# Weighted expert groups: a seven-product scheme for the first product, and matmuls in 64x64 pieces on two halves of the rows

## The chip, the cores and the metric

The kernel runs on one core of one Trainium2 chip. The metric is device time in microseconds, the median of the runs. The engines are TensorE (PE in the profile: matmuls, with their weight loads as PEld), VectorE (DVE), ScalarE (ACT), GpSimd (POOL) and SyncE (SP), which issues most DMAs.

## What is computed

An attention block with polynomial features makes `x` (4352 rows of 128). Then a mixture of eight experts works on it, with weights `P` from eight rounds of row and column normalisation. All of it is fp32.

```python
    logits = x @ w_gate
    ...
    for _ in range(8):
        P /= P.sum(1, keepdims=True) + 1e-09
        P /= P.sum(0, keepdims=True) + 1e-09
        P *= N / E
    out = np.zeros((N, D), dtype=np.float32)
    for e in range(E):
        h = np.maximum(x @ w1[e], 0.0)
        ye = h @ w2[e]
        out += P[:, e:e + 1] * ye
```

Here N = 4352, D = 128, E = 8, and the hidden width F = 1024. Two matrix products for each expert take nearly all the time: the first is `x @ w1[e]`, the second `h @ w2[e]`. As P is not negative, `P * relu(x @ w1)` is `relu((P * x) @ w1)`: a weighted group multiplies x by P ahead of the first product and then sums over the experts in PSUM.

## The kernel before

**Layout.** `xT` holds x transposed: 128 features on the partitions, tokens along the free axis. The first product puts hidden units on the partitions, the second puts output features there.

**Groups, items, blocks.** `groups` is a list of (first token, tile width, tiles, experts, weighted). The eight groups ahead of `PLAIN` are unweighted, two tiles wide, for experts 0 and 1; they run beside the attention and the routing. Then come five weighted groups of three tiles of 256 tokens (`NT3`), for experts 1 to 7 (the group at token 512: 2 to 7), and a last weighted group of two tiles. An *item* is a group with one expert. An item of a three-tile group has two *blocks*; a block is four of the eight slices of 128 hidden units. There are 34 such items and 68 such blocks; they are the three-tile stage, from 184.9 to 830.0 us.

**A three-tile block** (`four`, `twenty`). `first` (L906 to L920) makes, for each slice, two matmuls of 128x64 weights, one for each half of the array's columns, with 512 or 256 tokens, into one bank of PSUM, and ScalarE stores the relu to `hx` or `hb` in turn (L920). `sums` has VectorE form thirteen sums and differences of these slices (L980, L1000). The second product is a scheme of 20 products of half blocks of W2 and of 256 tokens in place of 24: `twenty` lists them, and `into` (L1107) adds them into four banks of PSUM over all experts of the group. The 16 needed sums of half blocks of W2 are made by GpSimd in the first weighted group (`sums_of_four`, L242), stored in DRAM, and loaded by the later groups.

**Order.** For PE, DVE and ACT the order is written out by hand: `steps` emits, for each step of a block, one `first`, then the sums that are due, then the second products of a block begun eight steps earlier (`LAG`). So first and second products alternate on PE. GpSimd's and SP's work is kept in program order where `keep_in_program_order` says so.

**Inputs of an item.** `prepare_x` loads the row of P for the expert, repeated on all partitions (a DMA from `pT`, L674), and GpSimd multiplies it with x into `xe` (L678). `prepare_w` loads W1, W2 and the forms of W2. Both run one item ahead.

**End of a group.** When a bank is complete, ScalarE copies it out (L820), and `part_of_twenty` combines the four copies: 23 additions on VectorE (`do`, L823), five copies between halves on ScalarE (L842), three transposes (L714), and the stores.

Of the kernel before, what the change touches and what calls it, by code (L numbers as in the profile page):

```python
# [10 lines left out]
F32 = mybir.dt.float32  # L11
# [39 lines left out]
def kernel(  # L51
# [32 lines left out]
    sk = ctx.enter_context(tc.tile_pool(name="sk", bufs=2))  # L84
# [5 lines left out]
    early = ExitStack()  # L90
    ld = early.enter_context(tc.tile_pool(name="ld", bufs=2))
# [94 lines left out]

    def load_w(e, sums=True, again=False):
# [6 lines left out]
    def sums_of_two(e, w2, again=False):  # L194

        ws = wpool.tile([P, 4, FO // 2, H2], F32, tag="ws", name="ws")
# [27 lines left out]
    FORMS = [n for ns, *_ in FOURS for n in ns]  # L224

    def sums_of_four(e, w2):
# [6 lines left out]
        def blocks(bs):  # L233
            b = w2[:, bs[0][1]::4, H2 * bs[0][0]:H2 * (bs[0][0] + 1)].unsqueeze(1)
            if len(bs) == 1:
                return b
            step = (bs[1][1] - bs[0][1]) * DM + (bs[1][0] - bs[0][0]) * H2
            return AP(tensor=b.tensor, offset=b.offset, ap=[b.ap[0], [step, 2], *b.ap[2:]])
# [10 lines left out]


# [320 lines left out]
    def routing():  # L571

        yield 5
# [52 lines left out]
    lower, upper = slice(0, H2), slice(H2, P)  # L626
# [28 lines left out]
    def prepare_w(j):  # L655
        g, e = items[j]
        three = groups[g][2] == 3
        if j == 0:
            loaded_w[j] = first_w
        elif items[j - 1][1] == e or not groups[g][4]:  # L660
            before = [i for i in range(j) if items[i][1] == e and i in loaded_w]
            loaded_w[j] = loaded_w[before[-1]] if before else load_w(e, False)
            if three and tiles_of(j - 1) == 2:
                loaded_w[j] = *loaded_w[j][0:2], sums_of_four(e, loaded_w[j][1])
        else:
            loaded_w[j] = load_w(e, not three, again=groups[g][4])
            if three:
                if g == len(groups) - 2 and e in groups[-1][3]:
                    sums_of_two(e, loaded_w[j][1], True)
                loaded_w[j] = *loaded_w[j][0:2], sums_of_four(e, loaded_w[j][1])  # L670
# [9 lines left out]
    def prepare_x(j):  # L680
# [3 lines left out]
        if not weighted:  # L684
            sources[j] = x
            return
        xe = weights_of(e, lo, t * n, "xe")
        for sl in (slice(0, 512), slice(512, 768)) if j == first_weighted else (slice(0, t * n),):
            weigh(xe[:, sl], x[:, sl], xe[:, sl])
        sources[j] = xe  # L690
# [123 lines left out]
    def part_of_twenty(g, k):  # L814
# [7 lines left out]
        def do(out, a, b, off=False):  # L822
            at_leisure(lambda: nc.vector.tensor_tensor(out, a, b, op=Alu.subtract if off else Alu.add))  # L823
# [12 lines left out]
        elif k == 3:  # L836
# [51 lines left out]
    def room_of(k):  # L888

        lo, n, t, _, weighted = groups[items[blocks[k][0]][0]]  # L890
        if t == 3:
            if "x" not in hs:
                hs["x"] = pools[0].tile([P, 25, NT3], F32, name="hx", bufs=1)
                hs["pqg"] = pools[0].tile([P, 3, NT3], F32, name="pqg", bufs=1)
# [59 lines left out]
    U4, U2, V3, V1, U1, V4, W1, W2, U3, BB, V2, W3, W4 = range(12, 25)  # L954

    def four(k):
        j, q = blocks[k]
        h = hs[k] = room_of(k)
        pqg = hs["pqg"]
        order = ((0, 0), (3, 0), (3, 1), (0, 1), (1, 0), (2, 0), (1, 1), (2, 1))  # L960

        def at(f, t):
            return 4 * t + f

        def step(c):
            f, last = order[c]
            if last:
                first(k, 4 * q + f, 2 * NT3, 3 * NT3, h[:, at(f, 2)], False)
            else:
                first(k, 4 * q + f, 0, 2 * NT3, h[:, f:f + 8:4], False)  # L970

        def places(*bs):
            if len(bs) == 1:
                return h[:, bs[0]]
            if bs[0] == bs[1]:
                return h[:, bs[0]:bs[0] + 1].to_broadcast([P, 2, NT3])
            return h[:, bs[0]:bs[1] + 1:bs[1] - bs[0]]

        def do(out, a, b, off=False):
            nc.vector.tensor_tensor(out if not isinstance(out, tuple) else places(*out), places(*a),  # L980
                                    places(*b) if isinstance(b, tuple) else b, op=Alu.subtract if off else Alu.add)

# [296 lines left out]
```

## Time and profile before

| | |
|---|---|
| median of the runs | 919.61 us (2 runs: 919.25 and 919.96) |
| the profiled execution: span from its first to its last instruction | 917.7 us |
| three-tile stage, 68 blocks | 184.9 to 830.0 us |
| granted TensorE clock | 1.00 throughout |
| DMA | 128 MB, 140 GB/s on average |

A row of the page's groups and of the list by form reads: line, engine, operation, written tile <- read tiles, partitions x elements, count, then busy us, mean ns of one, and idle time of the engine just before. A row of the timeline: start, length, engine, line, operation, tiles, shape, count of merged instructions, and in brackets the idle time before and what ended it. A row of a table by stretch: the stretch, its length, then for each engine its busy time and its number of instructions, the granted clock, the DMAs' share and their rate. The row of one tile's or line's instructions has the shortest, median and longest duration in ns. Every fp32 matmul shows as two records.

### The profile page before, as it was taken

To read this page: it belongs to the slowest core of one execution; us is meant where nothing else is said; L and a number is where in the kernel's file an instruction comes from. 1 tells how busy PE (TensorE), PEld (TensorE's weight loads), DVE (VectorE), ACT (ScalarE), POOL (GpSimd) and SP (SyncE) were. 2 spreads that over 40 slices of the span, in tenths; PEclk is the share of its full clock that TensorE was granted. 3 is DMA by queue.
4 is the path that set the end of the run, shared out by engine and by line. 5 is a ranking of instruction groups with operands and counts; after the bars stand their busy time and mean duration, and the time that the engine had idled before them with its cause. 6 is when DMAs were issued, how large, how long until landed. Compare 5 with 4: busy or idle time off the path is not lost.

```text
span 917.7 us, 18881 instructions
## 1 busy us (share of the span) xinstructions
PE 910.4 (99%) x7434; PEld 695.8 (76%) x7434; DVE 687.7 (75%) x1173; ACT 422.7 (46%) x918; POOL 210.4 (23%) x212
## 2 busy tenths in 40 slices
PE   9999999999999999999999999999999999999997
PEld 6777544466666688888888888888888888888997
DVE  7678699888876798766975666966667987678654
ACT  3355465554444454444544444544445444446443
POOL 3121100175545422200210011110100352340110
PEclk9999999999999999999999999999999999999999
DMA  9994100213445545534364343463434556552550
GB/s 250 307 276 165 54 1 1 70 64 110 161 142 152 172 133 158 182 110 146 115 173 148 110 150 110 122 200 120 140 113 165 148 161 190 164 192 92 150 158 13
DMA packets 91305, 128.15 MB, mean 140 GB/s; under 512 B 25392, under 2 KB 69504, under 8 KB 86480
## 3 DMA queue, kind: packets, MB, share of 16 engines
q1 hardware_dynamic: 88384, 121.42, 43.0%
q0 software_dynamic: 1600, 5.36, 2.0%
q8 instruction: 58, 0.95, 0.4%
q10 hardware_dynamic: 1232, 0.16, 0.1%
q14 instruction: 31, 0.25, 0.1%
HBM read 107.88 MB, written 19.05 MB: 138 GB/s over the span
## 4 chain that ended last, share of the span: by engine, by line
PE 96%; DVE 2%; ACT 1%; DMA 1%; issue 0%; SPq 0%; DVEq 0%; ACTq 0%
PE a L916 51%; PE s L1107 41%; PE a L347 1%; PE a L462 1%; DMA kx<-in_k_dram 1%; DVE hb L933 1%; PE a L314 0%; PE s L376 0%; PE a L426 0%; PE s L392 0%; DVE cs L602 0%; PE a L496 0%; PE a L392 0%; ACT hb L920 0%; DVE rs L596 0%
## 5 line engine op out<-in xcount | busy, mean ns | idle before, releaser
L916 PE MATMUL a<-xe,w 128*64 128x256 f32 (+1 forms) x2560 | 615.4, 470 | 0.0
L916 PEld LDWEIGHTS a<-xe,w 128*64 128x64 f32 x2560 | 306.3, 137 | 39.2 <-issue 1.6
L920 ACT ACTIVATE hb<-a 128x256 f32<-128x256 f32 (+4 forms) x408 | 195.1, 480 | 241.7 <-PE a L916 210.9
L1107 PE MATMUL s<-hb,ws 128*64 128x256 f32 (+3 forms) x1312 | 276.4, 395 | 0.2 <-DVE hb L933 0.2
L920 ACT ACTIVATE hx<-a 128x256 f32<-128x256 f32 (+1 forms) x360 | 167.3, 465 | 211.6 <-PE a L916 194.6
L1107 PE MATMUL s<-hx,ws 128*64 128x256 f32 x1280 | 253.6, 379 | 0.0
L1107 PEld LDWEIGHTS s<-hb,ws 128*64 128x64 f32 x1312 | 161.5, 137 | 67.9 <-issue 14.7
L980 DVE TENSOR_TENSOR hb<-hb 128x512 f32<-128x512 f32 (+1 forms) x204 | 138.3, 687 | 97.9 <-ACT hb L920 93.8
L678 POOL TENSOR_TENSOR xe<-xT,xe 128x768 f32<-128x768 f32 (+2 forms) x41 | 84.0, 2050 | 490.5 <-DMA xe<-pT 363.6
L1107 PEld LDWEIGHTS s<-hx,ws 128*64 128x64 f32 x1280 | 159.6, 137 | 48.3
L980 DVE TENSOR_TENSOR hx<-hx 128x512 f32<-128x512 f32 (+1 forms) x204 | 149.0, 741 | 59.1 <-ACT hx L920 54.1
L1107 PE MATMUL s<-hb,w 128*64 128x256 f32 (+3 forms) x536 | 120.3, 408 | 0.0
L916 PE MATMUL a<-xT,w 128*64 128x416 f32 (+3 forms) x512 | 119.9, 462 | 0.0
L1107 PE MATMUL s<-hx,w 128*64 128x256 f32 x384 | 81.8, 379 | 0.0
L933 DVE TENSOR_TENSOR hb<-hb 128x416 f32<-128x416 f32 (+7 forms) x84 | 59.9, 713 | 19.4 <-ACT hb L920 15.8
L1107 PEld LDWEIGHTS s<-hb,w 128*64 128x64 f32 x536 | 60.0, 137 | 17.4 <-issue 6.5
L916 PEld LDWEIGHTS a<-xT,w 128*64 128x64 f32 x512 | 49.5, 137 | 25.0 <-issue 15.6
L242 POOL TENSOR_TENSOR ws<-w 128x256 f32<-128x256 f32 (+1 forms) x70 | 61.1, 907 | 8.1 <-DMA w<-in_moe_w_dram 8.0
L933 DVE TENSOR_TENSOR hx<-hx 128x256 f32<-128x256 f32 (+1 forms) x65 | 37.2, 576 | 25.4 <-ACT hx L920 24.2
L1107 PEld LDWEIGHTS s<-hx,w 128*64 128x64 f32 x384 | 46.4, 137 | 4.4
L980 DVE TENSOR_TENSOR pqg<-hb 128x512 f32<-128x512 f32 x68 | 43.2, 676 | 0.0
L980 DVE TENSOR_TENSOR pqg<-hx 128x512 f32<-128x512 f32 x68 | 37.7, 594 | 0.0
(180 smaller groups left out, 489.8 us busy)
## 6 DMA issues: line engine op xcount, KB each, us to landing
w<-in_moe_w_dram SPq DMA_DIRECT2D x82, 512.0 KB, 5.5
ws<-ws SPq DMA_DIRECT2D x34, 1024.0 KB, 4.9
xe<-pT SPq DMA_DIRECT2D x34, 384.0 KB, 4.0
ws<-ws SPq DMA_DIRECT2D x12, 512.0 KB, 3.1
ph<-qa SPq DMA_DIRECT2D x12, 288.0 KB, 4.8
rb<-qb SPq DMA_DIRECT2D x3, 1152.0 KB, 7.6
pb<-pT SPq DMA_DIRECT2D x6, 384.0 KB, 8.6
kx<-in_k_dram SPq DMA_DIRECT2D x4, 544.0 KB, 5.0
```

The source lines that it names most:

```text
L242: tc.keep_in_program_order(nc.gpsimd.tensor_tensor(ws[:, c:c + len(ns)], blocks(x), blocks(y), op=Alu.subtract if off else Alu.add))
L347: nc.tensor.matmul(pv[64 * s:64 * (s + 1), i], kp[0:n, H * t + h].rearrange("p i j -> p (i j)"), vx[0:n, slots[h], t, :], start=(t == 0 an ...
L462: nc.tensor.matmul(pn[64 * s:64 * (s + 1), t, 2 * i:2 * i + 2].rearrange("p h d -> p (h d)"), ph[:, i, s, 64 * t:64 * (t + 1)], kvs[b % 2] ...
L678: tc.keep_in_program_order(nc.gpsimd.tensor_tensor(out, x, pb, op=Alu.mult))
L916: nc.tensor.matmul(ph[sl], loaded_w[j][0][:, P * f + H2 * s:P * f + H2 * (s + 1)], sources[j][:, lo:hi], start=True, stop=True, tile_posit ...
L920: nc.scalar.activation(out=out, in_=ph, func=Act.Relu)
L933: nc.vector.tensor_tensor(out, a, b, op=Alu.subtract)
L980: nc.vector.tensor_tensor(out if not isinstance(out, tuple) else places(*out), places(*a), places(*b) if isinstance(b, tuple) else b, op=A ...
L1107: nc.tensor.matmul(sums[g][i][H2 * s:H2 * (s + 1), n * place:n * (place + 1)], w, x, start=c == 1 and not seeded, stop=c == per, tile_posi ...
```

## The change

In the three-tile groups alone, both products are rearranged; the two-tile groups stay.

**First product.** It is taken as a product of 2x2x2 blocks: the features in two halves of 64 (partitions 0 to 63, `lower`, and 64 to 127, `upper`), four slices of hidden units as two pairs, the 768 tokens in two halves of 384 (`HALF`). Seven products replace eight. They need sums and differences of blocks of W1 and of x. Those of W1 are made once for each expert by GpSimd during the routing (`forms_of_first`: four subtractions of 512 columns for each of seven experts, with five loads and two stores) and kept in DRAM. Those of x come from `de`: `join_halves` makes once a group the sums of halves of x (`dg`), and `prepare_x` multiplies both x and `dg` by P (two products of 768 columns) and subtracts halves (two of 384 columns, one of them on 64 partitions).

**Pieces.** Every matmul of both products now has 64x64 weights: 64 rows of the array by 64 columns. The rows 0 to 63 and 64 to 127 are two streams, each with seven first products of 384 tokens and ten pairs of second products of 256 tokens a block.

**Combining.** One of a pair of slices takes seven products in three banks. ScalarE copies one partial sum into another bank (`seed`) and one to SBUF (`m5`), VectorE adds `m5` twice, with its other input in PSUM, and ScalarE makes four relus, one of them from SBUF. So a block has 12 ScalarE operations and 4 new VectorE additions of 384 columns. The ten VectorE operations of the sums for the second product stay.

**Order.** `middle` replaces `four` and the alternation of `steps` for the stage: each operation has a time within a block, blocks follow every `PERIOD`, and all are issued in the order of these times. The times only fix the order. Two streams must not be in one bank of PSUM at once; where a bank passes from one to the other, the matmul waits for a ScalarE or VectorE operation that shows that the other stream is done (`witness`).

**Elsewhere.** The 23 final additions of a group move from VectorE to GpSimd. W1 arrives in four DMAs, two of them of stored forms; W2 and its forms are loaded at their own item's start (`second_weights`), W1 and the weighted x in the item before. The queue of the two-tile stage is emptied before the middle starts, and the last group starts after the middle's last product.

```diff
+    def forms_of_first(e, t):
...
+        less(g[lower, :, 0], g[lower, :, 1], u[lower, :, 1])
+        less(g[upper, :, 1], g[upper, :, 1], g[upper, :, 0])
+        less(u[:, :, 0], u[:, :, 1], u[:, :, 0])
+        less(u[:, :, 1], u[:, :, 0], g[:, :, 1])
...
+    def first_weights(j):
...
+        tc.keep_in_program_order(nc.sync.dma_start(out=w1[upper], in_=moe_w1[e][upper]))
...
+        tc.keep_in_program_order(nc.sync.dma_start(out=w[lower, :, 0], in_=x[lower, :, 0]))
+        tc.keep_in_program_order(nc.sync.dma_start(out=w[lower, :, 1], in_=t3))
+        tc.keep_in_program_order(nc.sync.dma_start(out=wf, in_=made))
...
+    def second_weights(j):
...
+        loaded_w[j][2:] = w2, sums_of_four(e, w2)
...
+            px = weights_of(e, lo, t * n, "px")
+            xe, de = (pools[0].tile([P, 2, HALF], F32, tag=a, name=a) for a in ("xe", "de"))
+            weigh(xe.rearrange("p t n -> p (t n)"), x, px)
+            weigh(de.rearrange("p t n -> p (t n)"), joined[g], px)
+            for sl, a in ((slice(0, P), de), (lower, xe)):
+                i = 0 if a is de else 1
+                tc.keep_in_program_order(nc.gpsimd.tensor_tensor(a[sl, i], a[sl, 0], a[sl, 1], op=Alu.subtract))
...
+    def join_halves(g):
...
+        for sl, c in ((upper, slice(0, 2 * HALF)), (lower, late_)):
+            tc.keep_in_program_order(nc.gpsimd.tensor_tensor(d[sl, c], d[sl, c], x[sl, c], op=Alu.add))
...
-            at_leisure(lambda: nc.vector.tensor_tensor(out, a, b, op=Alu.subtract if off else Alu.add))
+            at_leisure(lambda: tc.keep_in_program_order(
+                nc.gpsimd.tensor_tensor(out, a, b, op=Alu.subtract if off else Alu.add)))
...
+    PERIOD = 8.83
...
+    def middle():
...
+        def product(out, row, w, c0, x, start, stop):
+            r = ROWS[row]
+            for s in range(2):
+                sl = slice(H2 * s, H2 * (s + 1))
+                nc.tensor.matmul(out[sl], w[r, c0 + H2 * s:c0 + H2 * (s + 1)], x[r], start=start, stop=stop,
+                                 tile_position=(H2 * row, H2 * s), skip_group_check=True)
...
+            product(*{1: (bx, 0, w1, fa, xe[:, 0], True, False), 2: (bx, 1, w1, fa, xe[:, 0], False, True),
+                      3: (by, 1, w1, fb, de[:, 0], False, True), 4: (b, 1, wf, fb, xe[:, 1], False, True),
+                      5: (by, p, wf, fa, de[:, 1], True, True), 6: (b, 0, wf, fb, de[:, 0], False, True),
+                      7: (b, 0, w1, fb, xe[:, 1], False, True)}[n])
...
+        def vector(k, p, what):
+            ins = nc.vector.tensor_tensor(by if what == 1 else raw(k, p, 1, 1), bb[p], m5s[p], op=Alu.add)
...
+        SUMS = ((9.2, (U4, U2), (at(0, 0), at(3, 0)), (at(0, 1), at(3, 1)), False),
...
+                (17.95, (W4,), pqg[:, 2], (V2,), True))
+        FIRST = {1: (0, 4.31), 2: (2.37, 7.1), 3: (4.53, 8.83), 4: (7.75, 11.85), 5: (1.72, 6.46), 6: (2.37, 6.9),
+                 7: (4.95, 9.475)}
+        SCALAR = {"seed": (1.3, 5.2), "m5": (2.63, 7.36), "11": (3.28, 8.0), "12": (5.5, 9.73), "22": (6.55, 11.13),
+                  "21": (8.66, 12.75)}
+        VECTOR = {1: (3.3, 7.9), 2: (5.86, 10.38)}
+        SECOND = ((14.43, 14.86, 16.37, 15.3, 16.8, 20.67, 21.1, 21.53, 17.23, 18.96),
+                  (18.74, 19.17, 21.33, 19.6, 21.76, 23.7, 26.06, 27.1, 22.83, 23.26))
...
+            if q == 0:
+                if n:
+                    add(t + 1.2, second_weights, j)
...
+                    add(t + 3.9, first_weights, j + 1)
+                    add(t + 4, prepare_x, j + 1)
```

A time pair in `FIRST`, `SCALAR` and `VECTOR` belongs to the two pairs of slices of a block; the two rows of `SECOND` to the two streams.

319 lines of the change are left out of this document (228 added, 91 removed).

## The prediction

> **What bounds the kernel now.** I read the page first: busy shares, then the chain of work that ended last.
>
> ```profile
> span 917.7 us, 18881 instructions
> ...
> PE 910.4 (99%) x7434; PEld 695.8 (76%) x7434; DVE 687.7 (75%) x1173; ACT 422.7 (46%) x918; POOL 210.4 (23%) x212
> ...
> PE 96%; DVE 2%; ACT 1%; DMA 1%; issue 0%; SPq 0%; DVEq 0%; ACTq 0%
> ...
> PE s L1107 <- DVE hb L933: 0.2, 1, 0.2
> ```
>
> The chain is TensorE from end to end, and the list of waits (last line) holds one TensorE wait before these two products, of 0.2 us. Since a busy PE need not be PE at its peak, I looked next at the order of time inside one three-tile block, at a stretch with 384 columns, and at the busy time by stage.
>
> ```profile
> 499.59 1.18 PE L916 MATMUL a<-xe,w 128*64 128x512 f32 x4
> 500.44 0.75 PE L1107 MATMUL s<-hx,ws 128*64 128x256 f32 x4
> 500.88 0.75 PE L916 MATMUL a<-xe,w 128*64 128x256 f32 x4
> ...
> 509.06 0.59 PE L916 MATMUL a<-xe,w 128*64 128x512 f32 x1
> ...
> 181.66 0.82 PE L916 MATMUL a<-xT,w 128*64 128x384 f32 x4
> 182.30 0.82 PE L1107 MATMUL s<-hb,w 128*64 128x384 f32 x4
> ```
>
> A pair of fp32 matmuls (two column halves, two records each) starts every 0.85 us at 512 columns (499.59 to 500.44), 0.44 at 256, 0.64 at 384. The starts are the cadence; the 1.18 and 0.75 include a tail that overlaps the next pair. A block has 4 pairs of 512 and 4 of 256 in the first product and 10 of 256 in the second: 4 x 0.85 + 14 x 0.43 = 9.4, and the trace repeats itself after 9.47 (499.59 to 509.06). So TensorE streams without a hole, and fewer columns would be less time, if the other engines keep up.
>
> ```profile
> core 0: us, PE busy (x) PEld busy (x) DVE busy (x) ACT busy (x) POOL busy (x), PEclk, DMA share, GB/s
> 184.89:318.22 133.33, 133.33 (x1001) 87.55 (x997) 105.38 (x145) 58.94 (x121) 74.27 (x77) 1.00 0.42 131
> 564.63:697.31 132.68, 132.68 (x1012) 107.59 (x1010) 91.30 (x168) 58.69 (x122) 17.61 (x8) 1.00 0.45 138
> ...
> 184.89:829.98 645.09, 41.26 (x92) 1.00 0.46 144
> ```
>
> The first two lines are the first and the fourth weighted group, 14 blocks each. The last is VectorE's busy time in the additions of the groups' ends (L823) over the whole three-tile stage of 68 blocks, 645.1 us. VectorE is busy 6.52 us a block in the fourth group and 7.53 in the first, where GpSimd makes the forms of W2.
>
> **What TensorE saves.** A block's first product becomes 14 pairs of 384 columns with 64 rows, 7 on each half of the rows; the second, 10 pairs of 256 on each half. One half takes 7 x 0.645 + 10 x 0.431 = 8.82 us. That is the block if the halves run side by side. Rows bearing on this:
>
> ```profile
> 8.74 1.99 PE L376 MATMUL s<-qT,wq 64*128 64x512 f32 x8
> ...
> 10.66 0.84 PEld L347 LDWEIGHTS a<-v,kp 128*64 128x64 f32 x26 [0.76 <-PE s L376]
> ```
>
> Eight records of 512 columns on alternating row halves take 1.99 us, where one after another they would take 8 x 0.427 = 3.4: the halves do overlap. 26 weight loads begin within 0.84 us, 0.03 each, and the new block has 136, 4.4 us of it. I take 8.83. Against 9.48: 0.65 x 68 = 44 us less. From above: 44.
>
> **What VectorE gets.** It keeps the ten sums of the second product, loses the groups' ends, and gains four additions of 384 columns a block that read PSUM.
>
> ```profile
> L477 DVE TENSOR_TENSOR rd<-a,rc 128x384 f32<-128x384 f32 x9 | 5.0, 558 | 0.3
> ...
> L920 ACT ACTIVATE hb<-a 128x384 f32<-128x384 f32 x32 | 15.6, 493 | 16.0 <-PE a L916 11.4 <-PE s L1107 2.6 <-ACT hb L920 1.4
> ```
>
> L823 is 41.26 / 5 / 14 = 0.59 us a block. So 6.52 - 0.59 + 4 x 0.558 = 8.16 of 8.83, or 16.3 of 17.66 an item (two blocks, one expert). ScalarE's 12 operations of 0.49 make 5.9: it fits.
>
> **What GpSimd gets, and what that does to VectorE.** An item had one GpSimd product of 768 columns. It now has two, and two subtractions of 384; each group's 23 final additions also move there, and the joining of the halves.
>
> ```profile
> L678 POOL TENSOR_TENSOR xe<-xT,xe x41: 1037/1940/4135, 180.3 to 887.6; 128x768 f32<-128x768 f32 x33, 128x512 f32<-128x512 f32 x7, 128x256 f32<-128x256 f32 x1
> ...
> 360.07 1.86 POOL L678 TENSOR_TENSOR xe<-xT,xe 128x768 f32<-128x768 f32 x1 [1.62 <-DMA xe<-pT]
> ...
> 360.17 2.31 DVE L980 TENSOR_TENSOR hx<-hx 128x512 f32<-128x512 f32 x1
> ...
> 17.94 0.82 DVE L384 TENSOR_TENSOR ph<-ph,s 128x288 f32<-128x288 f32 x2 [0.27 <-PE s L376]
> ...
> 18.30 0.74 POOL L203 TENSOR_TENSOR ws<-w 128x256 f32<-128x256 f32 x1
> ```
>
> A sum of 512 columns issued 0.1 us behind a GpSimd product lasts 2.31 us and ends 0.55 after that product. The same operation between 342.86 and 343.47, below, has 0.68. It is held for the whole GpSimd operation. Two additions that read PSUM (L384) take 0.82 together, though GpSimd starts in the middle of them. So new GpSimd time turns into VectorE time, except where VectorE is idle or reads PSUM. An item's new GpSimd time is 1.94 + 2 x 0.97 (half of 768 columns, estimated) = 3.88 us; four PSUM additions may cover 0.28 each, leaving 3.0: 19.4. The 23 additions hold about 0.6 each (the ten operations of the first group below average 0.89, waiting included), 2 us an item; they are short enough to go beside PSUM additions, so I charge a quarter, 0.5. Joining, four times 1.94 + 0.97 over 34 items, half charged, 0.17. Together 20.0 us an item where TensorE wants 17.66. In the first group the forms of W2 add what they add now, (7.53 - 6.52) x 2 = 2.0; I charge 1.7: 21.7.
>
> 27 x 20.0 + 7 x 21.7 = 692 us for the stage.
>
> Bounds. From below, all GpSimd time is hidden and TensorE sets 17.66: 600. From above, by turns:
>
> ```profile
> 260.20 8.92 POOL L242 TENSOR_TENSOR ws<-w 128x256 f32<-128x256 f32 x10 [1.06 <-DMA w<-in_moe_w_dram]
> ...
> 260.39 2.09 DVE L980 TENSOR_TENSOR pqg<-hb 128x512 f32<-128x512 f32 x2
> 262.40 1.21 DVE L980 TENSOR_TENSOR hb<-hb,pqg 128x512 f32<-128x512 f32 x1
> ...
> 341.11 4.12 POOL L678 TENSOR_TENSOR xe<-xT,xe 128x768 f32<-128x768 f32 x1 [15.62 <-DMA xe<-pT]
> ...
> 342.86 0.68 DVE L980 TENSOR_TENSOR hx<-hx 128x512 f32<-128x512 f32 x1
> 343.47 0.43 DVE L714 STREAM_TRANSPOSE yt<-y 128x256 f32<-128x256 f32 x1
> 343.83 1.68 DVE L980 TENSOR_TENSOR hx<-hx 128x256 f32<-128x256 f32 x1
> ```
>
> At 260 to 269 the two engines alternate, each sum 1.21 instead of 0.69. Now that cost TensorE nothing, because VectorE had a fifth of its time free and the products that use its sums run a block behind. In the change's tables the first PSUM addition ends at 3.3 + 0.56 and the product that needs it stands at 4.53: 0.7 us of room. Strict turns over the item's four GpSimd operations (5.5 us held) put VectorE about 4.2 us behind: 21.9 an item, 745 in all. At 341 it went otherwise: GpSimd issued and VectorE's chain of sums went on before it for 2.4 us, until the transpose with a single input. The Trainium skill (SBUF — State Buffer, "Who interferes with whom") says that issue order decides and the loser fully blocks; by that alone the sum would be 745. The 341 rows speak against it, and for operations entering at PSUM additions, as I charged.
>
> **The smaller terms.** The stage's seams: now the last two-tile products run between the first weighted ones. The new code first empties the old queue, starts its second products 14.43 us after its first block, and the last ends at 27.5: between 0 and 27.5 - 8.83 = 18.7 us, I take 8 (first products move up until ScalarE's 5.9 a block stops them). Preparing the forms of W1: 28 GpSimd subtractions of 512 columns, about 1.3 us each by the same scale, before 184.89:
>
> ```profile
> 91.80:184.89 93.09, 92.87 (x634) 44.75 (x631) 79.21 (x143) 51.64 (x106) 7.55 (x9) 1.00 0.11 31
> ...
> w<-in_moe_w_dram SPq DMA_DIRECT2D x82, 512.0 KB, 5.5
> ws<-ws SPq DMA_DIRECT2D x34, 1024.0 KB, 4.9
> ```
>
> GpSimd is nearly free there and VectorE has 14 us left, with the routing chain to serve: 0 to 10, I take 2. Their loads and stores share SP's queue with the W loads, at a DMA share of 0.11: nothing. An item's DMA grows by half a megabyte on a share of 0.45; second_weights waits on SP for the form buffer, freed 1.0 us into the item by the tables, and holds the next item's W1 and weights behind it, which are wanted over 16 us later and land in 5.5: nothing. The stream-to-stream waits on ScalarE and VectorE results leave 0.35 us or more by the tables and go with the lateness already charged.
>
> Sum: 917.7 - 645.1 + 692 + 8 + 2 = 974.6 for the span. The runs' median, 919.6, is 1.9 above the span, so 976. This likeliest case's own range is 940 to 1015, from an item of 19 to 21.
>
> **Rivals.**
> *GpSimd's operations hide* (0.24). Each slips into an idle gap or beside a PSUM addition, lateness stays under 0.7 us, and TensorE sets the pace: 917.7 - 44 + 8 + 2 + 1.9 = 886. For it: the 341 rows, and 8 PSUM additions an item. Against: one such opening is 0.56 us, a product 1.9, and VectorE is 92% full before any of this. It decides if the item stays under 18.96, its length now.
> *Half hides* (0.18): about 18.7 an item, 636 + 8 + 2, thus 920, no change.
> *Strict turns* (0.11): the 260 to 269 rows in every item, each VectorE sum behind a whole GpSimd operation: 745 + 7 x 2 for the first group, 917.7 + 114 + 10 + 1.9 = 1044. The Trainium skill's rule above would have it so.
> *The halves do not run side by side* (0.02): 17.6 a block, over 1400. L376 speaks against it.
>
> **How the numbers follow.** The forecast has 0.45. A measurement of this kernel tells 2% from no change, 18 us: faster is below 901, slower above 938. Faster: 0.24. Same: 0.18 and a little of the forecast's edge. Slower: the rest. The range must take in the 886 case, and leaves out most of strict turns: 884 to 1035.
>
> **What would show it.** A block cadence of 8.83 in the records of 384 columns, VectorE idle before PSUM additions for TensorE: the first rival. A cadence near 10, TensorE waiting on VectorE's PSUM additions, VectorE's sums of 512 columns averaging over 0.9 and GpSimd busy 40% or more of the stage: the forecast. Waits on ScalarE or on the stream-to-stream results, or a gap above 10 us at the seams, would make me wrong in the reason; GpSimd operations that hold VectorE's sums for less than their length would make me wrong in the size.

## The result, and the profile after

The changed kernel takes 1141.1 us at the median (1140.6 and 1141.6), against 919.6 before: 1.2415 times as long [1.2378, 1.2451]. The profiled execution has a span of 1138.8. The forecast was 976, in a range that ended at 1035.

The first lines of the page, and its chain of waits:

```profile
span 1138.8 us, 28477 instructions
...
PE 978.1 (86%) x11794; PEld 652.2 (57%) x11794; DVE 906.4 (80%) x1330; ACT 532.8 (47%) x1201; POOL 494.1 (43%) x466
...
PE 49%; DVE 24%; DMA 8%; POOL 7%; issue 6%; ACT 4%; SPq 1%; POOLq 0%; DVEq 0%; ACTq 0%
```

TensorE carried 96% of the chain and has 49% now. Yet no other engine is full: VectorE is busy for 80% of the span. So this isn't one bound that took another's place; engines wait for each other in turn. Busy time by stage (columns as before: TensorE, weight loads, VectorE, ScalarE, GpSimd, granted clock, DMA share):

```profile
core 0: us, PE busy (x) PEld busy (x) DVE busy (x) ACT busy (x) POOL busy (x), PEclk, DMA share, GB/s
91.80:218.94 127.14, 106.50 (x665) 47.90 (x660) 110.42 (x147) 55.45 (x115) 60.70 (x49) 0.95 0.41 114
218.94:391.02 172.08, 140.19 (x1766) 91.54 (x1768) 143.39 (x190) 78.44 (x171) 88.31 (x91) 0.92 0.40 120
529.65:689.17 159.52, 142.49 (x1909) 102.97 (x1901) 134.04 (x199) 81.15 (x177) 67.12 (x52) 0.94 0.50 145
844.78:1049.50 204.72, 163.55 (x2086) 108.54 (x2084) 144.43 (x216) 88.42 (x202) 94.58 (x83) 0.92 0.46 134
```

The first line is the work from 91.80 to the first weighted three-tile product; that product starts at 218.94, where it started at 184.89. GpSimd's 7.55 us there have become 60.70. The other three are the first, the third and the last group of the stage. The stage as a whole runs from 218.94 to 1049.50: 830.6 us, 24.4 an item, where it had 645.1 and 18.97. What follows it takes 89.3 (87.7 before). So 34 of the 221 us are lost ahead of the stage, 185 in it, 1.6 behind it.

The stage's inner work, first VectorE, then GpSimd, over the same 7 us:

```profile
612.35 0.57 DVE L1174 TENSOR_TENSOR a<-a,hb 128x384 f32<-128x384 f32 x1 [0.44 <-PE a L1136]
613.26 2.04 DVE L1189 TENSOR_TENSOR hx<-hx 128x512 f32<-128x512 f32 x1 [0.35 <-ACT hx L1169]
615.23 3.44 DVE L1189 TENSOR_TENSOR hb<-hx 128x512 f32<-128x512 f32 x2
618.59 0.55 DVE L1174 TENSOR_TENSOR hb<-a,hb 128x384 f32<-128x384 f32 x1
```

```profile
612.94 1.82 POOL L726 TENSOR_TENSOR xe<-xT,px 128x768 f32<-128x768 f32 x1 [11.82 <-DMA px<-pT]
614.72 2.27 POOL L726 TENSOR_TENSOR de<-dg,px 128x768 f32<-128x768 f32 x1
617.06 1.32 POOL L745 TENSOR_TENSOR de<-de 128x384 f32<-128x384 f32 x1
618.35 1.17 POOL L745 TENSOR_TENSOR xe<-xe 64x384 f32<-64x384 f32 x1
```

The item's four GpSimd operations come in one burst, and the two engines take turns: three sums that last 0.68 each when nothing else runs take 5.5 us. The additions that read PSUM (L1174) keep their 0.55 to 0.57 throughout. But the second of them, due 2.56 us behind the first by the change's tables, comes 6.24 behind it, because in the order of VectorE it stands behind the held sums. And TensorE's list of waits now begins with that line:

```profile
PE a L1136 <- DVE hb L1174: 43.6, 20, 10.6
PE s L1308 <- DVE hb L1006: 16.3, 8, 9.1
```

### The profile page after: what moved, and what is told of

It reads as the page before. It is cut to its first block, busy times and chain, and to the rows that moved or that the text cites. A ratio compares the mean times of both kernels' runs of the same rounds, so it can differ in the third digit from the quotient of the medians.

```text
span 1138.8 us, 28477 instructions
## 1 busy us (share of the span) xinstructions
PE 978.1 (86%) x11794; PEld 652.2 (57%) x11794; DVE 906.4 (80%) x1330; ACT 532.8 (47%) x1201; POOL 494.1 (43%) x466
## 3 DMA queue, kind: packets, MB, share of 16 engines
q8 instruction: 93, 1.52, 0.6%
## 4 chain that ended last, share of the span: by engine, by line
PE 49%; DVE 24%; DMA 8%; POOL 7%; issue 6%; ACT 4%; SPq 1%; POOLq 0%; DVEq 0%; ACTq 0%
PE s L1308 21%; PE a L1136 19%; DVE hb L1189 8%; DMA px<-pT 6%; PE a L989 6%; DVE hx L1189 6%; DVE hb L1006 3%; POOL xe L726 2%; ACT hb L1169 1%; POOL y L897 1%; DVE hb L1174 1%; DVE a L1174 1%; POOL de L726 1%; DVE kept L813 1%; PE a L375 1%
## 5 line engine op out<-in xcount | busy, mean ns | idle before, releaser
L1308 PE MATMUL s<-hb,ws 64*64 64x256 f32 (+4 forms) x2400 | 335.6, 397 | 16.6 <-DVE hb L1006 16.3
L1136 PE MATMUL a<-xe,w 64*64 64x384 f32 x1640 | 335.9, 513 | 13.8 <-POOL xe L726 12.3
L1308 PE MATMUL s<-hx,ws 64*64 64x256 f32 (+1 forms) x2368 | 323.5, 401 | 21.1 <-DMA ws<-ws 11.7
L1308 PEld LDWEIGHTS s<-hb,ws 64*64 64x64 f32 (+1 forms) x2400 | 174.7, 137 | 82.9 <-issue 30.9
L1308 PEld LDWEIGHTS s<-hx,ws 64*64 64x64 f32 (+1 forms) x2368 | 168.5, 141 | 67.6 <-issue 15.0
L1136 PE MATMUL a<-de,wf 64*64 64x384 f32 x1088 | 192.2, 499 | 3.4 <-POOL r L897 2.0
L1136 PE MATMUL a<-xe,wf 64*64 64x384 f32 x544 | 119.0, 516 | 49.7 <-DVE hb L1174 43.6
L1308 PE MATMUL s<-hb,w 64*64 64x256 f32 (+4 forms) x808 | 146.6, 403 | 7.9 <-DVE hb L1189 5.5
L1136 PEld LDWEIGHTS a<-xe,w 64*64 64x64 f32 x1640 | 122.2, 139 | 53.8 <-POOL xe L726 17.1
L1136 PE MATMUL a<-de,w 64*64 64x384 f32 x544 | 120.4, 521 | 12.0 <-DVE a L1174 12.0
L1174 DVE TENSOR_TENSOR a<-a,hb 128x384 f32<-128x384 f32 x136 | 76.2, 561 | 46.8 <-PE a L1136 41.6
```

The source lines that it names most:

```text
L1136: nc.tensor.matmul(out[sl], w[r, c0 + H2 * s:c0 + H2 * (s + 1)], x[r], start=start, stop=stop, tile_position=(H2 * row, H2 * s), skip_grou ...
L1174: ins = nc.vector.tensor_tensor(by if what == 1 else raw(k, p, 1, 1), bb[p], m5s[p], op=Alu.add)
L1308: mm = nc.tensor.matmul(sums[g][i][H2 * s:H2 * (s + 1), n * place:n * (place + 1)], w, x, start=c == 1 and not seeded, stop=c == per, tile ...
```

## The experiments

Three theories stood at the start. *Port*: GpSimd's reading holds VectorE's sums of two SBUF inputs, and the lateness passes to TensorE. *Queue*: the weighted inputs come late, through SP's queue (the wait of 11.82 us for px above). *Streams*: the 64x64 pieces, or the waits between the two streams, are slower than the tables have it. An item is two blocks, one expert; its length is taken from its first 64x384 matmul to that of the next. Line numbers shift by some lines from kernel to kernel. Each experiment is a single run, beside one of the kernel before, which gave 918.4 to 919.9. *The middle twenty* are the 8th to the 27th item; *the last seven* reach to the stage's last 64x64 matmul.

**One product.**

```
-            xe, de = (pools[0].tile([P, 2, HALF], F32, tag=a, name=a) for a in ("xe", "de"))
+            xe = pools[0].tile([P, 2, HALF], F32, tag="xe", name="xe")
             weigh(xe.rearrange("p t n -> p (t n)"), x, px)
-            weigh(de.rearrange("p t n -> p (t n)"), joined[g], px)
-            for sl, a in ((slice(0, P), de), (lower, xe)):
...
-            sources[j] = xe, de
+            sources[j] = xe, xe
```

> Leaves out, in the three-tile stage, the second GpSimd product (de) and both subtractions of each item; xe stands in for de. GpSimd's burst per item falls from 6.6 to 1.9 us. Theory port (GpSimd operations hold VectorE's sums): an item falls from 24.4 us on average to about 19.5, the time to about 975 (940 to 1010). Theory queue (the weighted inputs arrive late through SP and the DMAs): only the burst's own 4.7 us leave the chain from load to first product, so at most the same gain, and TensorE then still waits for loads. Theory streams (the two row halves or their waits are the limit): no change, 1130 to 1145.

1024.7: 116 us less, though above the 940 to 1010 of the port theory. Items of 18.5 to 21 in the middle groups.

**No product**, and the final additions on VectorE.

```
+            xe = px.rearrange("p (t n) -> p t n", t=2)
+            sources[j] = xe, xe
...
-            at_leisure(lambda: tc.keep_in_program_order(
-                nc.gpsimd.tensor_tensor(out, a, b, op=Alu.subtract if off else Alu.add)))
+            at_leisure(lambda: nc.vector.tensor_tensor(out, a, b, op=Alu.subtract if off else Alu.add))
```

> Leaves out all four GpSimd operations of each item (the loaded row of P stands in for xe and de) and makes the groups' final additions on VectorE again. Theory port: nothing on GpSimd is left in the groups 2 to 5 but the joins and the kept parts; the item comes to 17.7 to 18.5 us, VectorE then 17.5 busy of it, time 900 to 950. Theory queue: the loads still come at the same point of the item, 12 us in, which is early enough without a burst: 900 to 950 too, but with TensorE waiting for the loads. Theory streams: blocks stay above 10 us, time above 1100.

961.7. Busy time over a stretch of 11 items, and two additions of PSUM one block apart:

```profile
471.00:670.00 199.00, 197.66 (x2998) 163.11 (x2994) 178.30 (x349) 130.96 (x282) 6.91 (x4) 1.00 0.61 178
```

```profile
547.23 0.57 DVE L1168 TENSOR_TENSOR a<-a,hb 128x384 f32<-128x384 f32 x1 [0.39 <-PE a L1130]
...
556.06 0.57 DVE L1168 TENSOR_TENSOR a<-a,hb 128x384 f32<-128x384 f32 x1 [0.44 <-PE a L1130]
```

TensorE is busy 197.7 of 199.0 us at a granted clock of 1.00, VectorE waits for it, and the block shown takes 8.83. Most items of the middle stand at 17.7; with the longer ones among them the middle twenty average 18.4. The streams theory falls: TensorE does what the tables say. But 961.7 is still slower than before, with all of an item's GpSimd products away. The stage starts at 214.3; the items of the first group, where GpSimd makes the forms of W2, take 18.1 to 23.2 (143.0 in all for seven, against 123.6); the last takes 26.4, with a wait of 5.4 for the forms of W2 to land.

**The final additions alone** go back to VectorE (the second half of the diff above).

> Undoes one part: the 23 final additions of a group on VectorE again. Theory port: 115 GpSimd operations of about 1 us no longer hold VectorE, VectorE gets 115 of 0.42: 1090 (1060 to 1125). Theory queue: GpSimd reaches the next item's products sooner by up to 3 us in five items of seven: 1070 to 1140. Theory streams: no change.

1109.9, 31 us less. 24 of them are in the last seven items and 7 behind the stage; the middle twenty are only 2 shorter in all, and the first seven take 3 more. Beside the burst, the additions cost next to nothing in the middle.

**No sums for the forms of W1.** The four `less(...)` lines of `forms_of_first` are left out, and the second store takes `g[lower, :, 1]`; the loads (four an expert, not five) and both stores stay.

> Leaves out the 28 GpSimd subtractions that make the forms of W1 (the raw halves are stored instead; all loads and stores stay). Theory port: the 34 us by which the three-tile stage starts later come from VectorE behind these subtractions: the stage starts near 190 instead of 219, time 1110 (1105 to 1120). If the added loads and stores are the cause: the stage still starts near 219.

1114.6, 26 us less. The stage starts at 201.9 instead of 218.9: 17 of the 34. The other 17 are not the subtractions. Ahead of the stage stand also the first item's products and the join of the halves, before which GpSimd was idle for 30.25 us, by the profile until a load of stored forms (`wf<-wf`) landed.

**P first.** The row of P for the next item is loaded ahead of W2's forms.

```
+                if tiles_of(j + 1) == 3:
+                    add(t + 0.1, load_px, j + 1)
                 if n:
                     add(t + 1.2, second_weights, j)
```

> One part moved: the next item's row of P is loaded at the item's start, ahead of the loads of W2 and its forms that hold SP's queue. Nothing is left out. Theory queue: GpSimd's burst starts up to 8 us earlier in the item, the waits of the first products for xe go, an item loses 2 to 5 us: 1000 to 1070. Theory port: the burst holds VectorE just as long wherever it stands: less than 1 us an item, 1110 to 1145.

1125.9. In the middle the burst now starts some 3.6 us into an item instead of 11 or 12, no TensorE wait is put down to GpSimd's products any more, and the items still take 21 to 26: the middle twenty average 23.6 where they had 22.7, so they became slower. In the middle the queue theory falls. At both ends of the stage it has a part: the first seven items are 17 us shorter and the last seven 19.

**Writing alone.** GpSimd's four operations are replaced by four fills, which read nothing.

```
-            weigh(xe.rearrange("p t n -> p (t n)"), x, px)
...
+            for sl in (slice(0, 768), slice(0, 768), slice(0, 384), slice(384, 768)):
+                tc.keep_in_program_order(nc.gpsimd.memset(px[:, sl], 0.5))
```

> Replaces the four GpSimd operations of an item by four that write the same numbers of columns (768, 768, 384, 384) into the loaded row of P, without reading anything, and this stands in for the weighted inputs: the chain from load over four GpSimd operations to the first product stays, the reads go. Theory port (it is the reading that holds VectorE's sums of two SBUF inputs): items near those of the run without products, 17.7 to 19, time 960 to 1000 (the final additions are still on GpSimd). Theory queue, or GpSimd's mere presence: items stay above 21, 1050 to 1140.

996.3, with items of 17.7 to 20.8 in the middle groups. The groups of that kernel:

```profile
L741 POOL MEMSET px<- 128x768 f32 x68 | 50.1, 737 | 371.1 <-DMA px<-pT 281.1 <-PE a L1133 78.7 <-PE s L1305 9.4
...
L741 POOL MEMSET px<- 128x384 f32 x68 | 26.4, 418 | 2.0
```

```profile
L1186 DVE TENSOR_TENSOR hx<-hx 128x512 f32<-128x512 f32 x136 | 101.8, 749 | 12.5 <-ACT hx L1166 12.4
```

The chain load, GpSimd, TensorE is kept, with the same wait for P. VectorE's sums of 512 columns average 749 ns, where the same line of the changed kernel (`hx<-hx`) averages 896. That mean still has the forms of W2 in it, which GpSimd reads as before. In the stretch from 220 to 840 us, the 39 sums of 512 columns that met a fill and no other GpSimd operation lasted 0.69 us at most, where the 113 that met a reading operation in the changed kernel averaged 1.39. It is the reading that holds them, in line with the Trainium skill (SBUF — State Buffer, "Who interferes with whom"), by which GpSimd contends with a VectorE operation of two SBUF inputs when it reads, not when it only writes. The fills are also shorter than the products, so the time of the run doesn't measure the reading alone. But one reading product of 1.9 us an item (the run with one product) left the middle twenty at 19.6, and four fills of 2.3 us together at 18.8.

**The burst in the kernel before.** The kernel before gets a second product and two subtractions an item, into a tile that nobody reads.

```
+        if t == 3:
+            de = pools[0].tile([P, 3 * NT3], F32, tag="de", name="de", bufs=1)
+            weigh(de, x, xe)
+            for sl in (slice(0, P), slice(0, H2)):
+                tc.keep_in_program_order(nc.gpsimd.tensor_tensor(de[sl, 0:384], de[sl, 0:384], de[sl, 384:768],
+                                                                 op=Alu.subtract))
```

> The kernel before, with the burst added: behind each item's product GpSimd makes a second one of 768 columns and two subtractions of 384, into a tile that nothing reads. Theory port with tight places in the order: VectorE's sums are held as in the changed kernel (512 columns at 0.9 us and more), but nothing of TensorE waits so closely: 919 to 935. If VectorE's total time is what counts (6.5 + 2.4 of 9.5 us a block): also 919 to 935. If GpSimd's reads slow TensorE or its loads directly: above 960.

961.0: 43 us more than the kernel before beside it (918.4), and over what was expected. Most items keep their 19.0 us under the burst; 21 to 26 stand in the first group and at the groups' ends, where forms of W2 or final additions come on top. The same three operations, left out in the run with one product, were worth 1141.1 - 1024.7 = 116 us in the new order. The length of GpSimd's work doesn't set its price alone.

**The store from GpSimd's queue.**

```
-            nc.sync.dma_start(out=stored[e], in_=ws)
+            (nc.gpsimd if pool else nc.sync).dma_start(out=stored[e], in_=ws)
```

> One line of the changed kernel: the store of the two-tile forms in the last three-tile group is issued from GpSimd's queue, where it follows the operations that make the tile, not from SP's, where it waited up to 23 us for them with the next item's loads behind it. Theory: the last group's items of 32, 27 and 42 us come down to the 22 to 24 of the others: 1105 (1095 to 1120). If the GpSimd work itself makes those items long: 1130 to 1141.

1125.1. In the changed kernel SP's waits had this line, in the last three-tile group:

```profile
SPq L211 <- POOL ws L208: 90.3, 6, 23.0
```

That is the store of the two-tile forms, waiting on SP for GpSimd with the next item's loads queued behind it. With it gone the group's items of 32, 27 and 42 us become 23 to 27, and the last seven take 182 us instead of 204. The first seven take 8 more, which leaves 16. It is not a loss of its own: the same wait shrinks with the final additions on VectorE (first line) and with P first (second line).

```profile
SPq L211 <- POOL ws L208: 69.6, 6, 14.6
SPq L211 <- POOL ws L208: 45.5, 6, 8.1
```

**All parts away**: no products, no form sums, final additions on VectorE, store on GpSimd's queue.

> Leaves out the GpSimd work of every item (the row of P stands for both weighted inputs), and the 28 subtractions that make the forms of W1; the 23 final additions of a group are on VectorE and the store of the two-tile forms is issued from GpSimd's queue. If the parts found so far are the whole loss: 961.7 of the run without products, less about 17 for the subtractions, less about 10 for the store, thus 925 to 945, with a stage near 34 x 17.7 = 602 but for the first group, where the forms of W2 are still made. The expected gain of 44 against the kernel before would then be seen in the stage and given back ahead of it and behind it. If something else than these parts slows the new order, it stays above 955.

938.4. Even so the kernel isn't faster than before. The stage starts at 197.7, 13 us late; the first group's items take 17 to 23; from there on nearly all take 17.7 or 19 to 20.

**Three mends together**: final additions, store, P first.

> Computes everything. The final additions are on VectorE, the store of the two-tile forms on GpSimd's queue, the row of P loaded ahead of W2's forms. Alone they gave 31, 16 and 15 us. If they are separate losses they add up: 1070 to 1090. If each only shifts the same lateness from one cause to the next, 1095 to 1110. The items of the later groups should still stand at 21 or more, since the burst is still in each.

1111.9, no better than the best of the three alone (1109.9). They don't add up, because all three shorten the same stretch: the last seven items take 204 us in the changed kernel, 180, 182 and 185 with one of the mends, and 187 with all three. And P first, which gains 17 us in the first seven, makes the middle twenty slower here too (23.2 against 22.6 with the additions alone). Something about the burst itself had to be found.

**The burst spread**, in eight pieces, each tied to the VectorE operation ahead of an addition that reads PSUM (shown without the allocation and the piece's own operation; P is loaded and the halves joined an item earlier).

```
-                    add(t + 4, prepare_x, j + 1)
+                    for i, at_ in enumerate((1.55, 3.3, 5.86, 7.9, 10.38, 12.13, 14.69, 16.73)):
+                        add(t + at_ - 0.005, piece, j + 1, i)
...
+            tc.add_manual_dep(ins.ins, pieces["last"].ins.name, SYNC, reason="beside the addition")
```

> Computes everything. The burst of an item is cut into eight pieces (six products of 256 columns, two subtractions of 384), and each piece waits for the VectorE operation ahead of one of the item's eight additions that read PSUM, so that it starts beside that addition; the final additions are on VectorE and the store is on GpSimd's queue. GpSimd reads as much as with the whole burst. If reading costs VectorE only while a sum of two SBUF inputs is due, each piece of 0.65 to 1.0 us is covered for 0.56 of it, about 2 us of 7 remain in an item: items of 17.7 to 19 outside the first group, 950 to 1000 in all. If GpSimd's reading costs its length wherever it stands, or if the waits between the two engines cost more than the port, it stays at 1060 to 1100.

1027.1, 85 less than with the whole burst, but over the 950 to 1000 that were expected; 14 items of the middle (501.4 to 773.2) average 19.4. GpSimd's pieces and VectorE in the same stretch:

```profile
563.67 0.73 POOL L1163 TENSOR_TENSOR de<-dg,px 128x256 f32<-128x256 f32 x1 [0.82 <-DVE hb L1218]
566.12 0.73 POOL L1163 TENSOR_TENSOR de<-dg,px 128x256 f32<-128x256 f32 x1 [1.72 <-DVE hb L1218]
```

```profile
563.51 0.56 DVE L1202 TENSOR_TENSOR a<-a,hb 128x384 f32<-128x384 f32 x1
564.41 1.63 DVE L1218 TENSOR_TENSOR hb<-hb 128x512 f32<-128x512 f32 x3 [0.34 <-ACT hb L1197]
566.01 0.56 DVE L1202 TENSOR_TENSOR hx<-a,hb 128x384 f32<-128x384 f32 x1
566.48 1.52 DVE L1218 TENSOR_TENSOR hb<-hb 128x512 f32<-128x512 f32 x2
```

The piece at 563.67 ends as VectorE's wait for ScalarE does, and costs nothing. That at 566.12 holds the two sums behind its addition for 1.52 - 1.36 = 0.2 us.

**The same pieces without ties**, issued together.

```
-            tc.add_manual_dep(ins.ins, pieces["last"].ins.name, SYNC, reason="beside the addition")
...
-                        add(t + at_ - 0.005, piece, j + 1, i)
+                        add(t + 4, piece, j + 1, i)
```

> Computes everything; the kernel of the spread pieces with their ties taken out: the same eight pieces of the same sizes, issued one behind the other 4 us into the item, with nothing to wait for but their inputs. If the place of a piece (beside an addition that reads PSUM) is what made the spread kernel fast, this goes back to 1075 to 1110, like the whole burst with the same mends. If shorter operations, or P loaded an item earlier, made it fast, it stays at 1020 to 1045.

1032.8: it is not the ties that made it fast. They are worth 6 us by these two runs; the sums are held again and it hardly matters.

**Uncut.** The six products of 256 columns are two of 768 again, all else as in the run before.

```
+            if i % 4 == 0:
+                ins = nc.gpsimd.tensor_tensor(a.rearrange("p t n -> p (t n)"), x, pieces["px"], op=Alu.mult)
```

> Computes everything; the kernel with the pieces and no ties, with its six products of 256 columns put together again to two of 768, everything else as there (the row of P an item earlier, de ahead of xe, the joining an item earlier, the final additions on VectorE, the store on GpSimd's queue). If the length of a single GpSimd operation sets how late VectorE's sums become, this goes to 1085 to 1115, with TensorE waiting for VectorE's additions again, 2 us and more at a time, and its granted clock under 0.96. If the earlier start of the burst or the earlier row of P made the cut kernel faster, it stays at 1025 to 1050.

1049.3: nor is it the cutting, which is worth 16 us. This kernel has the burst of the three mends, unshortened, and is 63 us faster. What is left between the two is that P and the join come an item earlier, and that de is made ahead of xe, so that the burst starts 0.6 us into an item.

**xe first again**, the order of the change, all else as in the uncut kernel.

```
-                    for i, at_ in enumerate((1.55, 3.3, 5.86, 7.9, 10.38, 12.13, 14.69, 16.73)):
+                    for i in (4, 0, 3, 7):
```

> Computes everything; the uncut kernel (1049.3) with one edit: the four GpSimd operations in the change's own order, the product into xe first, then de and the two subtractions. The buffer of xe is released by the last product of the block before, some 3 us into the item, that of de at its start, so the burst begins about 3 us later in the item; the row of P is still loaded an item earlier. If the burst's place among the eight additions decides, it goes to 1090 to 1115, with a burst that starts 3.3 to 4.1 us into the items. If the earlier row of P or the earlier joining made the difference to 1111.9, it stays at 1045 to 1060.

1112.8. That is the whole difference: the order of the four operations, and with it a start of the burst three microseconds later, is worth 63 us. The order and the place changed together; no run starts the burst early with xe first. VectorE and GpSimd, with xe first:

```profile
643.91 0.57 DVE L1199 TENSOR_TENSOR a<-a,hb 128x384 f32<-128x384 f32 x1 [0.41 <-PE a L1141]
644.38 0.41 DVE L902 TENSOR_TENSOR y<-y,kept 128x256 f32<-128x256 f32 x1
644.89 5.49 DVE L1215 TENSOR_TENSOR hb<-hb 128x512 f32<-128x512 f32 x3
650.30 0.55 DVE L1199 TENSOR_TENSOR hx<-a,hb 128x384 f32<-128x384 f32 x1
```

```profile
644.47 2.00 POOL L1157 TENSOR_TENSOR xe<-xT,px 128x768 f32<-128x768 f32 x1 [9.44 <-PE a L1141]
646.43 2.26 POOL L1157 TENSOR_TENSOR de<-dg,px 128x768 f32<-128x768 f32 x1
648.77 1.32 POOL L1160 TENSOR_TENSOR de<-de 128x384 f32<-128x384 f32 x1
```

```profile
648.15 0.61 PE L1338 MATMUL s<-hb,ws 64*64 64x256 f32 x4
650.90 0.54 PE L1141 MATMUL a<-xe,wf 64*64 64x384 f32 x2 [2.14 <-DVE hx L1199]
```

And the uncut kernel, with de first:

```profile
662.19 0.56 DVE L1201 TENSOR_TENSOR hb<-a,hb 128x384 f32<-128x384 f32 x1 [0.21 <-PE a L1141]
662.66 2.42 DVE L1217 TENSOR_TENSOR hb<-hb 128x256 f32<-128x256 f32 x2
665.00 0.55 DVE L1201 TENSOR_TENSOR a<-a,hb 128x384 f32<-128x384 f32 x1
665.59 1.54 DVE L902 TENSOR_TENSOR y<-m,z 64x256 f32<-64x256 f32 x1
```

```profile
661.55 2.11 POOL L1159 TENSOR_TENSOR de<-dg,px 128x768 f32<-128x768 f32 x1 [12.88 <-PE a L1141]
663.74 1.07 POOL L1162 TENSOR_TENSOR de<-de 128x384 f32<-128x384 f32 x1
665.03 1.82 POOL L1159 TENSOR_TENSOR xe<-xT,px 128x768 f32<-128x768 f32 x1 [0.23 <-PE a L1141]
```

With xe first the burst is let go by a TensorE product (the last that reads the old xe) and lands on the three sums that stand between the block's first addition of PSUM and its second. The second addition comes 6.39 us behind the first, and the fourth product of the block, which adds to the bank that this addition reads, waits 2.14 with TensorE idle. So it goes in all the middle twenty: in the block with the burst the second addition comes 6.6 us behind the first on average, in the item's other block 2.6. With de first the burst finds two sums of 256 columns (2.42 us together) between two additions 2.81 apart, and the second addition of the block comes 4.3 behind the first on average. The two kernels' windows over the same stretch, the first line with xe first, the second with de first:

```profile
501.00:637.70 136.70, 117.49 (x1562) 84.20 (x1558) 119.41 (x185) 67.21 (x147) 44.35 (x27) 0.90 0.51 139
```

```profile
501.00:637.70 136.70, 129.53 (x1834) 91.52 (x1830) 131.99 (x214) 77.39 (x171) 50.33 (x31) 1.00 0.60 165
```

VectorE is busy for 87% of the stretch in the slower kernel and for 97% in the faster one: the slower is not held up by too much work for VectorE, but by the place of the held work. A second loss rides on the first. The granted clock is 0.90 with the waits and 1.00 without. The Trainium skill (TensorE: Matmul & The Clock Gate, "HAM oscillation — how this bites in real kernels") has the clock fall at idle gaps of over some 3.4 us. Here it falls behind shorter ones: between 416 and 791 us it goes down again and again in the slower kernel, whose longest TensorE wait there is 3.2 us, and not in the faster, whose longest is 2.3 and whose others stay under 1.3. In the spread kernel it went to one half for 3.4 us right behind an idle gap of 1.42 (TensorE's row, then the table's, where the clock is the third number from the end):

```profile
539.74 0.69 PE L1341 MATMUL s<-hx,w 64*64 64x256 f32 x2 [1.42 <-issue]
```

```profile
539.60:543.00 3.40, 3.26 (x24) 2.23 (x28) 3.40 (x6) 0.93 (x2) 2.82 (x3) 0.50 0.14 46
```

What decides that one gap brings the clock down and another doesn't is not shown. How much of the 63 us is the clock's was not separated either; by the mean granted clock of the two spans (0.939 of 1110.6 us, 0.972 of 1047.4) an estimate has 38 us as the most that it can be.

## Why the prediction was wrong

The direction was right, and by the engine that it named; the size was not, and 1141 lies outside the range. Taken by its own terms, 130 of the 165 us missed lie in the stage and its seams (830.6 against 692 + 8), 32 in the preparation ahead of it (34 against 2), 1.6 behind it.

- *TensorE, 8.83 a block.* Right: 17.7 in most items without products, the halves side by side. Of the 1.3 us an item that this gains, about half was seen: with all parts away the middle twenty average 18.3, against 18.97 before. What the longer items among them wait for was not taken apart.
- *VectorE's share and what a GpSimd operation does to it.* Right in the mechanism: sums of two SBUF inputs are held while GpSimd reads (1.39 us on average for 512 columns, 0.68 alone), additions from PSUM aren't (0.54 to 0.57, all 272 of them). The turns of 260 to 269 came in most bursts.
- *20.0 us an item.* **This is the step that failed.** It charged GpSimd's operations by their length, as serial VectorE time, and set 20.0 against TensorE's 17.66, as if VectorE were going to be full. The item took 24.4, with VectorE at 80%. By the starts of the items the stage's 130 us are 54 in the middle twenty (22.7 each against 20.0), 20 in the first seven (172 against 7 x 21.7) and 57 in the last seven with the seam behind them (204.7 against 140 + 8). The price of a held sum depends on which addition stands behind it and how much room that one has. I named the room of a block's first addition (0.7 us) and used it only for the upper bound; the addition that the held sums stand before is the second, with 7.75 - 5.86 - 0.56 = 1.3 us by the tables, and it came 3.7 us late in the item shown (6.24 behind the first instead of 2.56). Where the burst begins early in the item, the middle twenty of the uncut kernel average 20.4: there the charge nearly fits. With xe first, the change's own order, they average 23.3. In the changed kernel itself the burst starts where P lands, mostly 11 to 12 us into an item. Counted from the item's second block, which is due 8.83 us in, that is about the place that the burst has in the first block when it starts at 3.6; the second block's two additions are 5.3 us apart on average, the first block's 2.6. P first moves the burst between these two places, and in the middle it cost 0.9 us an item.
- *Strict turns, 1044.* The nearest rival, at 0.11, and the better one: the 341 rows, taken against it, were an exception (in the three-tile stage of the changed kernel no GpSimd product of 768 columns took over 2.4 us). It too counted only time on VectorE, at 21.9 an item, and fell short by 97.
- *The final additions at a quarter*, 0.5 an item or 17 us: moving them back gave 31, but not where they were charged. The middle twenty gained 2 us; 24 came in the last seven, where the same mend shortens SP's wait for GpSimd, and 7 behind the stage.
- *The first group, 1.7 an item for the forms of W2.* That is 12 us for seven items. Without products they still took 143.0, 19 us above TensorE's time.
- *Preparation 2, at most 10.* It was 34, the largest miss among the small terms. The subtractions account for 17. I compared them with VectorE's idle time and left out that GpSimd's own queue then runs join, products, forms of W2 one behind the other, with VectorE's last two-tile work held under them. The 17 that remain were not taken apart further.
- *SP's queue at nothing.* With the store away from it the last seven items were 23 us shorter, of the 57 missed there. I looked at `second_weights` and not at the store of `sums_of_two`, which waits for GpSimd on that queue; in the kernel before it already did, 55.9 us in six waits.
- *The clock* had no term. It was 1.00 before and 0.94 over the changed kernel's stage, by which, as an estimate, up to 0.06 x 831 = 50 of the stage's 185 us lost are the clock's. As it falls behind waits, it is taken here as their consequence and not as a cause of its own.
- *Stream-to-stream waits at nothing.* Right, as the kernel without products shows.

By the same terms the kernel without products would have been 917.7 - 645.1 + 34 x 17.66 + 8 + 2 + 1.9 = 885, or 897 with the 12 us for the forms of W2; it took 961.7. So 65 to 77 us of the miss are there without the burst, and the other 88 to 100 came with the burst and the final additions. The other 17 us of the late start and most of the first group's excess stay open.

No version that was run beats the kernel before. The spread pieces come nearest with the whole work done, at 1027: VectorE is then busy 133.1 of 136.7 us, and the late start and the first and last groups remain.

## What to carry to other kernels

Work that holds another engine has a place as well as a length: find which instruction stands behind the held ones, who waits for it, and how much room the order leaves it. When several engines are set on a table with half a microsecond of room, look at what lets a burst go (a buffer, a load), since that fixes where it lands; here, making one operand ahead of the other was worth 63 us. And before adding up mends that were measured one at a time, look at where each one saved its time: three that all shortened the last group were worth no more together than the best of them alone.

## What the hardware showed that was not expected

GpSimd's operations issued back to back don't always take turns with VectorE. At the start of the stage, VectorE first, then GpSimd:

```profile
200.13 4.80 DVE L813 TENSOR_TENSOR kept<-z,m 64x384 f32<-64x384 f32 x1
```

```profile
197.63 3.35 POOL L763 TENSOR_TENSOR dg<-dg,xT 64x768 f32<-64x768 f32 x2 [30.25 <-DMA wf<-wf]
200.94 1.81 POOL L726 TENSOR_TENSOR xe<-xT,px 128x768 f32<-128x768 f32 x1
202.71 1.79 POOL L726 TENSOR_TENSOR de<-dg,px 128x768 f32<-128x768 f32 x1
204.58 1.19 POOL L745 TENSOR_TENSOR de<-de 128x384 f32<-128x384 f32 x1
```

One VectorE operation of 384 columns, issued under a GpSimd addition (of the join), lasted 4.80 us while two whole products went ahead of it, to end 0.35 into the third operation; at 613 the two engines alternated. What decides between the two cases was not tried.
